# Squaring on ScalarE and adding a mask by matmul in a fused attention and mixture-of-experts kernel

## The chip, the cores and the metric

One Trainium2 chip, one core. The metric is the device time of one execution in microseconds; each figure for a kernel is the median of its runs.

## The reference

The function has three parts in a row, all in float32 at the interface.

1. Windowed attention over q, k, v of shape (4, 8, 576, 64): scores are q times k transposed over sqrt(64), a position sees itself and the 63 before it, everything else is masked; softmax, then times v. The result is laid out as 2304 tokens of 512 values.
2. A dense block: `h = x @ w_in` (512 to 2048), `g = max(h, 0)**2`, `x = g @ w_out` (2048 to 512). Its two weight matrices come as 64-bit floats.
3. A routed block of 8 experts: a token whose `x @ w_skip` is above 0 goes to the expert with the largest of `x @ w_gate`, and gets `x + p * (max(x @ w1[e], 0) @ w2[e])`, p being the softmax of the gate at that expert; other tokens pass through.

## The kernel before

**Tiles.** There are 18 tiles t of 128 tokens; two make a chunk c of 256 tokens (nine chunks). Attention works on tiles and on groups g of four heads (two groups for each tile, four for each chunk). The dense block works in units (c, j): `l1(c, j)` computes a 256-wide slice j of the hidden layer for the 256 tokens of chunk c, and `l2(c, j)` adds its contribution to the two output accumulators of the chunk. There are 8 slices, so 72 units. Float32 products are made of three matmuls of rounded parts, "hi times hi", "hi times lo", "lo times hi" (`mm3`, L424 to L426), so each activation and each weight is split into a high part (type float32r) and the remainder.

**One unit.** `l1` runs 24 matmuls into one of two PSUM banks named `h`. ScalarE (ACT) takes the relu into `r` (L437), which frees the bank. Then ACT squares r into the high part `gh` (L443), VectorE (DVE) squares r in place (L444) and subtracts gh to give the low part `gl` (L445). `l2` runs two units later (12 matmuls of 512 columns, `acc`).

**One attention group.** `at_qk` runs four score matmuls of 128 columns each (L245) into one bank: one of the two banks `h` (printed as `s`) for the chunks 0 and 1, one of the two banks `a` from chunk 2 on. DVE then adds the mask, scales by -1/8 and takes the running minimum in one operation for each of the four heads (L257); its output goes to SBUF (`e`) and its minimum to `nmx`. ACT takes four exponentials from there with `nmx` as bias (L263), DVE adds 1e-9, inverts and scales (L266 to L269). `at_tr` transposes (L277), ACT copies (L279), `at_pv` multiplies by v (L295) and splits the result into `xt` (L303, L304). The groups of chunks 0 and 1 are numbered 0 to 7 below.

**Conversion of the dense weights.** `conv_next` handles one of 32 half-blocks: ACT scales the high words (L202), GpSimd (POOL) clips (L203), DVE shifts and merges the bits in three operations (L205, L207, L209), ACT casts to the high part (L214), POOL subtracts to the low part (L215) and the next load is issued. The first ones run among the attention of chunks 0 and 1; the others run one behind each half unit, while the units of chunks 0 and 1 alternate, and the attention of chunk 2 runs in the last units of that stage. From unit 16 on (chunks 2 to 8) no conversion is left.

**Order.** Each engine has one queue and runs it in order. Outside two stretches written by hand (the last units, and the experts) a planner orders the instructions of each engine by costs that it estimates. Masks are made on POOL by `setup_masks`, `mask_of(t)` picks the two 128-wide pieces for a tile; ten warm-up matmuls (L563) run before the first scores. SP's queue issues the loads.

Of the kernel before, what the change touches and what calls it, by code (L numbers as in the profile page):

```python
# [10 lines left out]
BF16 = mybir.dt.bfloat16  # L11
I32 = mybir.dt.int32
U32 = mybir.dt.uint32
AF = mybir.ActivationFunctionType
ALU = mybir.AluOpType
AX = mybir.AxisListType
# [3 lines left out]
P = 128  # L20
# [4 lines left out]
CT = 2  # L25
# [11 lines left out]
QK_H = (0, 1)  # L37
WARM = 10
NST = 3
LOADN = 3  # L40
EWS = (3, 0, 0)
LATE = (0,)
# [12 lines left out]
HUGE = 3.0e38  # L55
# [6 lines left out]
def body(ctx, tc, qt_d, kt_d, vw_d, wi_d, wo_d, w9_d, w9r_d, w1_d, w2_d, out):  # L62
    nc = tc.nc
    pool = lambda name, bufs, **kw: ctx.enter_context(tc.tile_pool(name=name, bufs=bufs, **kw))

    def scoped(*specs):
        stack = ExitStack()
        return [stack.enter_context(tc.tile_pool(name=n, bufs=b, **kw)) for n, b, kw in specs], stack
# [13 lines left out]
    (kv,), kv_stack = scoped(("kv", 1, {}))  # L82
    (st, kv2), st_stack = scoped(("st", NST, {}), ("kv2", 1, {}))
    kvs = (kv, kv2)
# [10 lines left out]
    def sm():  # L95
        return sp.tile([P, 512], F32, tag="sm", name="sm")

    ident = const.tile([P, P], F32, name="ident")
    mask = const.tile([P, 4, P], F32, name="mask")
    tri = const.tile([P, P], BF16, name="tri")  # L100
    ones = const.tile([P, P], BF16, name="ones")
    w9 = const.tile([P, KD, 10], F32, name="w9")
# [7 lines left out]

    def setup_masks():
        make_identity(nc, ident)
        nc.gpsimd.memset(mask, 0.0)
        for h0 in (0, 64):
            m = mask[h0:h0 + 64]
            for i in (0, 1, 3):
                nc.gpsimd.affine_select(
                    out=m[:, i, :], in_=m[:, i, :], pattern=[[1, P]], compare_op=ALU.is_gt,
                    fill=-HUGE, base=0, channel_multiplier=-1)
            nc.gpsimd.affine_select(  # L120
                out=m[:, 2, :], in_=m[:, 2, :], pattern=[[1, P]], compare_op=ALU.is_ge,
                fill=-HUGE, base=-WIN, channel_multiplier=0)
            nc.gpsimd.affine_select(
                out=m, in_=m, pattern=[[0, 4], [-1, P]], compare_op=ALU.is_ge,
                fill=-HUGE, base=WIN, channel_multiplier=1)

    def setup_routing():
        nc.gpsimd.memset(ones, 1.0)
        nc.gpsimd.memset(tri, 1.0)
        nc.gpsimd.affine_select(  # L130
            out=tri, in_=tri, pattern=[[1, P]], compare_op=ALU.is_gt,
            fill=0.0, base=0, channel_multiplier=-1)
        nc.gpsimd.iota(io8i, pattern=[[1, NE]], base=0, channel_multiplier=0)
        nc.gpsimd.tensor_copy(out=io8, in_=io8i)
        nc.gpsimd.iota(route[:, :, 0], pattern=[[P, NT]], base=0, channel_multiplier=1)
        nc.gpsimd.memset(ohsum[:, 0, :], 0.0)
        fill = sm().bitcast(I32)
        nc.gpsimd.memset(fill, FAR)
        nc.scalar.dma_start(
            out=tab_v.rearrange("p r c -> p (r c)"), in_=fill[:, 0:2 * ROW])  # L140
        nc.scalar.dma_start(out=w9, in_=w9_d)
# [3 lines left out]
    def half_of(t):  # L145
        return t % 2 if t < 3 * CT else 0
# [15 lines left out]
    def load_next(t, load):  # L162
        n = t + 2 if t < 3 * CT - 1 else t + 1
        if t != 3 * CT - 1 and n < NT:
            load(n)
# [51 lines left out]

    e_t = {}

    def mask_of(t):  # L220
        off = 0
        for blk in range(2):
            if (2 * t + blk) % (S // WIN) == 0:
                off = 2 if blk == 0 else 1
        return mask[:, off:off + 2, :].rearrange("p a b -> p (a b)")

    p_t, pt_t, xt_t = {}, {}, {}

    def bank(role, t, g):
        c, i = divmod(t, CT)  # L230
        if role == "qk" and c in QK_H:
            return ps_h.tile([P, 512], F32, tag="h", name="s")
        if role == "pv" and c < 2:
            p_ = acc_pool.get(c, ps_acc)
            return p_.tile([P, DM], F32, tag=f"acc{g}", name="xp")
        return psa()

    def at_qk(t, g):
        s = bank("qk", t, g)
        qp, k_ = qpad[half_of(t)], kt_t[t]  # L240
        for pi in range(2):
            for blk in range(2):
                u = 2 * pi + blk
                pr = 2 * g + pi
                nc.tensor.matmul(  # L245
                    s[:, u * P:(u + 1) * P],
                    lhsT=qp[:, 2 * pr + blk].rearrange("p a b -> p (a b)"),
                    rhs=k_[:, pr, 64 * blk:64 * blk + P],
                    start=True, stop=True)
        if g == 1:  # L250
            load_next(t, load_qk)
        ef = sm()
        e = ef.rearrange("p (a b) -> p a b", a=4)
        nmx = small.tile([P, 4], F32, tag="nmx", name="nmx")
        mk = mask_of(t)
        for u in range(4):
            nc.vector.tensor_tensor_reduce(  # L257
                out=e[:, u, :], in0=s[:, u * P:(u + 1) * P],
                in1=mk[:, u % 2 * P:(u % 2 + 1) * P], scale=-1.0 / 8.0, scalar=HUGE,
                op0=ALU.add, op1=ALU.min, accum_out=nmx[:, u:u + 1])  # L260
        sums = small.tile([P, 4], F32, tag="sum", name="sum")
        for u in range(4):
            nc.scalar.activation(  # L263
                out=e[:, u, :], in_=e[:, u, :], func=AF.Exp, bias=nmx[:, u:u + 1],
                scale=-1.0, accum_out=sums[:, u:u + 1])
        nc.vector.tensor_scalar(  # L266
            out=sums, in0=sums, scalar1=1e-9, scalar2=None, op0=ALU.add)
        nc.vector.reciprocal(out=sums, in_=sums)
        nc.vector.tensor_tensor(  # L269
            out=e, in0=e, in1=sums.unsqueeze(2).to_broadcast([P, 4, P]), op=ALU.mult)  # L270
        p_t[t, g] = e
# [151 lines left out]
    def mm3(out_ap, ah, al, bh, bl, start, stop):  # L423
        nc.tensor.matmul(out_ap, lhsT=ah, rhs=bh, start=start, stop=False)  # L424
        nc.tensor.matmul(out_ap, lhsT=ah, rhs=bl, start=False, stop=False)  # L425
        nc.tensor.matmul(out_ap, lhsT=al, rhs=bh, start=False, stop=stop)  # L426

    def l1(c, j):
        hp = ps_h.tile([P, 2, CTOK], F32, tag="h", name="h")
        xt = xt_t[c]  # L430
        for f in range(2):
            for k in range(KD):
                o = (k % 2) * 256 + f * P
                mm3(hp[:, f, :], wi_t[j, k // 2][:, 0, o:o + P], wi_t[j, k // 2][:, 1, o:o + P],
                    xt[:, 0, k, :], xt[:, 1, k, :], k == 0, k == KD - 1)
        r = rp.tile([P, 512], F32, tag="r", name="r")
        nc.scalar.activation(  # L437
            out=r, in_=hp.rearrange("p a b -> p (a b)"), func=AF.Relu)
        gh = gp.tile([P, 2, CTOK], F32R, tag="gh", name="gh")
        gl = gp.tile([P, 2, CTOK], F32R, tag="gl", name="gl")  # L440
        ghf = gh.rearrange("p a b -> p (a b)")
        glf = gl.rearrange("p a b -> p (a b)")
        nc.scalar.activation(out=ghf, in_=r, func=AF.Square)  # L443
        nc.vector.tensor_tensor(out=r, in0=r, in1=r, op=ALU.mult)  # L444
        nc.vector.tensor_tensor(out=glf, in0=r, in1=ghf.bitcast(F32), op=ALU.subtract)  # L445
        g_t[c, j] = (gh, gl)

# [91 lines left out]
    for c in range(NCH - 1):  # L539
        base = last[c] + LAG  # L540
        for i in range(2):
            t = c * CT + i
# [9 lines left out]
    if True:  # L552
# [17 lines left out]
        for _ in range(LOOK - 2):  # L570
            conv_load()
        setup_masks()
        setup_routing()
        acc_pool[1] = ps_s
# [31 lines left out]
        for u in range(n_u):  # L606
            if u == first[2]:
# [5 lines left out]
                    out=w9b, in_=w9r_d.unsqueeze(0).to_broadcast([P, NE + 1, DM]))  # L613
# [32 lines left out]
        def gather(ti, gw, kind, i=0, rows=NTOK):  # L646
            xg = xg_t[kind][i % len(xg_t[kind])]
            ins = nc.gpsimd.indirect_dma_start(
                out=xg, out_offset=None, in_=x2_d[0:rows],
                in_offset=bass.IndirectOffsetOnAxis(ap=ti, axis=0),  # L650
                bounds_check=rows - 1, oob_is_err=False)
            return ti, gw, xg, ins
# [11 lines left out]
        early = gather(near[:, 0:1], None, 2, rows=(NT - CT) * P)[2]  # L664
# [40 lines left out]
        with tc.manual_schedule():  # L705
# [13 lines left out]
            for _ in range(EWS[1]):  # L719
# [25 lines left out]
                out=id0, in0=pick, scalar1=float(FAR), scalar2=nearf, op0=ALU.add, op1=ALU.min)  # L745
# [4 lines left out]
                out=cnt, in0=pc[:, 0:NE], scalar1=float(P - 1), scalar2=None, op0=ALU.add)  # L750
            nc.vector.tensor_scalar(
                out=cnt, in0=cnt, scalar1=7, scalar2=None, op0=ALU.logical_shift_right)
# [98 lines left out]
        def static(e, xt):  # L851
            def fill(i):
                n, m = FILLS[i]
                if i == LOADN and e + 1 < NE:
                    for x in range(e + (e > 0), e + 2):
# [73 lines left out]
```

## Time and profile before

| what | value |
|---|---|
| runs | 708.15, 708.60, 708.81 us, median 708.6 |
| span of the profiled execution, first to last instruction | 705.2 us |
| PE, matmul busy | 659.6 us (94%) |
| DVE busy | 486.3 us (69%) |
| ACT busy | 307.8 us (44%) |
| POOL busy | 160.0 us (23%) |

The profile shows one execution. For it the trace gives the span alone; the runs are 3.4 us longer at the median, for what lies before the first and after the last instruction. Busy times are sums over instructions; PE's are overlapped and modelled at their ends, so that a busy PE is not one at its peak. [...]

### The profile page before, as it was taken

The page shows a single profiled execution, that of the slowest core. Times are in us where ns is not written, and L with a number is a line of the kernel's source. Part 1 is how long each engine was busy: PE and PEld are TensorE (multiplying, and loading weights), DVE is VectorE, ACT ScalarE, POOL GpSimd, SP SyncE. Part 2 cuts the span into 40 slices and gives each one's busy share as a digit, 9 for nine tenths or more (in the row PEclk, how much of TensorE's full clock was granted, in tenths as well). Part 3 has the DMA queues.
Part 4 walks back from the last instruction along what each step waited for, and adds up shares of the span by engine and source line. Part 5 has one row for each costly group of instructions (what it writes and reads, how often), then busy time and mean ns, then how long its engine had stood idle before and what let it go on. Part 6 is the DMA issues. An engine that isn't in the chain of part 4 may idle for free. (4 is left out here: it accounts for less than half of the span.)

```text
span 705.2 us, 12314 instructions
## 1 busy us (share of the span) xinstructions
PE 659.6 (94%) x4461; PEld 571.9 (81%) x4461; DVE 486.3 (69%) x1354; ACT 307.8 (44%) x729; POOL 160.0 (23%) x181
## 2 busy tenths in 40 slices
PE   6699798899999999999999999999999898998786
PEld 4588687679998989989989989889988676776564
DVE  5989999967937836935945945954755363399871
ACT  4775535443434424334334334344442352476541
POOL 5556555510100000000000000030011432226420
PEclk9889999999999999999999999999999999999998
DMA  8964543344123123022122121116335644288820
GB/s 288 265 214 140 166 128 122 113 127 166 35 66 98 38 61 98 31 68 78 51 68 78 51 68 66 62 61 238 122 115 190 218 153 141 73 287 323 284 72 8
DMA packets 51076, 88.70 MB, mean 126 GB/s; under 512 B 24046, under 2 KB 24302, under 8 KB 50864
## 3 DMA queue, kind: packets, MB, share of 16 engines
q1 hardware_dynamic: 47584, 83.38, 35.6%
q0 software_dynamic: 2976, 3.95, 1.7%
q8 instruction: 46, 0.75, 0.4%
q10 hardware_dynamic: 432, 0.32, 0.1%
q14 instruction: 38, 0.31, 0.1%
HBM read 79.07 MB, written 12.49 MB: 130 GB/s over the span
## 5 line engine op out<-in xcount | busy, mean ns | idle before, releaser
L424 PE MATMUL h<-xt,wi 128*128 128x256 f32 x576 | 166.5, 290 | 5.1 <-ACT r L437 3.1
L426 PE MATMUL h<-xt,wi 128*128 128x256 f32 x576 | 165.1, 288 | 0.0
L425 PE MATMUL h<-xt,wi 128*128 128x256 f32 x576 | 164.4, 287 | 0.0
L424 PEld LDWEIGHTS h<-xt,wi 128*128 128x128 f32 x576 | 111.4, 193 | 9.5 <-ACT r L437 4.1
L424 PE MATMUL acc<-wo,gh 128*128 128x512 f32 x288 | 115.7, 406 | 2.5 <-ACT wo L214 2.5
L426 PE MATMUL acc<-wo,gl 128*128 128x512 f32 x288 | 112.7, 393 | 1.4 <-DVE gl L445 1.4
L425 PE MATMUL acc<-wo,gh 128*128 128x512 f32 x288 | 113.6, 394 | 0.0
L425 PEld LDWEIGHTS h<-xt,wi 128*128 128x128 f32 x576 | 111.5, 194 | 2.5
L426 PEld LDWEIGHTS h<-xt,wi 128*128 128x128 f32 x576 | 111.5, 194 | 0.4
L444 DVE TENSOR_TENSOR r<-r 128x512 f32<-128x512 f32 x72 | 53.5, 744 | 62.2 <-ACT gh L443 62.0
L437 ACT ACTIVATE r<-h 128x512 f32<-128x512 f32 x72 | 42.3, 593 | 115.6 <-PE h L426 113.3
L506 DVE TENSOR_TENSOR e<-r,e 128x1024 fp32r<-128x1024 f32 x58 | 73.3, 1283 | 28.0 <-ACT e L504 21.5
L416 POOL DMA_INDIRECT tab_d<-route,posi x18 | 19.5, 1086 | 314.7 <-DVE mx L356 182.5
L335 DVE CUSTOM_DVE_ANT_0 prod<-sm,w9b 128x512 f32<-128x512 f32 x108 | 74.1, 686 | 0.2
L504 ACT CAST e<-r 128x1024 fp32r<-128x1024 f32 x58 | 59.6, 1050 | 27.6 <-PE h L426 14.4
L263 ACT ACTIVATE sm<-sm,nmx 128x128 f32<-128x128 f32 x144 | 56.1, 392 | 26.6 <-DVE nmx L257 25.1
L426 PEld LDWEIGHTS acc<-wo,gl 128*128 128x128 f32 x288 | 54.1, 188 | 13.4 <-DVE gl L445 2.1
L424 PEld LDWEIGHTS acc<-wo,gh 128*128 128x128 f32 x288 | 54.0, 189 | 12.4 <-ACT wo L214 3.4
L774 PE MATMUL h<-e,xh 128*128 128x512 f32 x176 | 49.4, 410 | 13.0 <-issue 6.6
L425 PEld LDWEIGHTS acc<-wo,gh 128*128 128x128 f32 x288 | 54.4, 189 | 8.4
L445 DVE TENSOR_TENSOR gl<-r,gh 128x512 fp32r<-128x512 f32 x72 | 53.3, 741 | 1.9
L774 PEld LDWEIGHTS h<-e,xh 128*128 128x128 f32 x176 | 31.9, 191 | 23.3 <-issue 14.9
(158 smaller groups left out, 1065.0 us busy)
## 6 DMA issues: line engine op xcount, KB each, us to landing
r<-in_w_dram SPq DMA_DIRECT2D x64, 512.0 KB, 5.4
v<-in_vw_dram SPq DMA_DIRECT2D x18, 512.0 KB, 3.6
ri<-in_wi_dram SPq DMA_DIRECT2D x16, 512.0 KB, 4.0
ro<-in_wo_dram SPq DMA_DIRECT2D x16, 512.0 KB, 3.5
k<-in_kt_dram SPq DMA_DIRECT2D x18, 384.0 KB, 3.9
qpad<-in_qt_dram SPq DMA_DIRECT2D x36, 128.0 KB, 3.2
x_d<-sm SPq DMA_DIRECT2D x17, 256.0 KB, 2.6
out_dram<-sm SPq DMA_DIRECT2D x17, 256.0 KB, 3.0
```

Source lines behind the costliest of these rows:

```text
L263: nc.scalar.activation(out=e[:, u, :], in_=e[:, u, :], func=AF.Exp, bias=nmx[:, u:u + 1], scale=-1.0, accum_out=sums[:, u:u + 1])
L335: nc.vector.tensor_tensor_reduce(out=prod, in0=x2_t[t], in1=w9b_t[0][:, j, :], scale=1.0, scalar=0.0, op0=ALU.mult, op1=ALU.add, accum_out ...
L416: nc.gpsimd.indirect_dma_start(out=tab_d, out_offset=bass.IndirectOffsetOnAxis(ap=posi, axis=0), in_=route[:, t, :], in_offset=None, bound ...
L424: nc.tensor.matmul(out_ap, lhsT=ah, rhs=bh, start=start, stop=False)
L425: nc.tensor.matmul(out_ap, lhsT=ah, rhs=bl, start=False, stop=False)
L426: nc.tensor.matmul(out_ap, lhsT=al, rhs=bh, start=False, stop=stop)
L437: nc.scalar.activation(out=r, in_=hp.rearrange("p a b -> p (a b)"), func=AF.Relu)
L444: nc.vector.tensor_tensor(out=r, in0=r, in1=r, op=ALU.mult)
L445: nc.vector.tensor_tensor(out=glf, in0=r, in1=ghf.bitcast(F32), op=ALU.subtract)
L504: nc.scalar.copy(out=hi, in_=raw)
L506: eng.tensor_tensor(out=lo, in0=raw, in1=hi.bitcast(F32), op=ALU.subtract)
L774: nc.tensor.matmul(hp[f], lhsT=xt[a][:, k * P:(k + 1) * P], rhs=w1_t[e, k][b][:, f * 512:(f + 1) * 512], start=(i == 0), stop=(i == len(m1 ...
```

## The change

In `l1` the DVE multiply is removed; ACT squares r in place and then copies r into gh with rounding. For chunks 0 to 2 (`EARLY`) a bf16 matmul of the identity with a bf16 mask writes the mask into the score bank first, the four score matmuls add to it, one DVE maximum reads the bank, ACT scales it by 1/8, and the exponentials read the bank. From chunk 3 on attention stays as it was, with a float32 mask now copied from the bf16 one.

```diff
+EARLY = (0, 1, 2)
...
+    identb = kv2.tile([P, P], BF16, name="identb")
     mask = const.tile([P, 4, P], F32, name="mask")
+    maskb = kv2.tile([P, 4, P], BF16, name="maskb")
...
         make_identity(nc, ident)
-        nc.gpsimd.memset(mask, 0.0)
+        nc.gpsimd.tensor_copy(out=identb, in_=ident)
+        nc.gpsimd.memset(maskb, 0.0)
         for h0 in (0, 64):
-            m = mask[h0:h0 + 64]
+            m = maskb[h0:h0 + 64]
...
+        nc.gpsimd.tensor_copy(
+            out=mask.rearrange("p a b -> p (a b)"), in_=maskb.rearrange("p a b -> p (a b)"))
...
-    def mask_of(t):
+    def mask_of(t, m):
...
-        return mask[:, off:off + 2, :].rearrange("p a b -> p (a b)")
+        return m[:, off:off + 2, :].rearrange("p a b -> p (a b)")
...
         qp, k_ = qpad[half_of(t)], kt_t[t]
+        early = t // CT in EARLY
+        if early:
+            nc.tensor.matmul(
+                s.rearrange("p (a b) -> p a b", a=2), lhsT=identb,
+                rhs=mask_of(t, maskb).unsqueeze(1).to_broadcast([P, 2, 2 * P]),
+                start=True, stop=False, skip_group_check=True)
...
-                    start=True, stop=True)
+                    start=not early, stop=True, skip_group_check=early)
...
-        mk = mask_of(t)
-        for u in range(4):
-            nc.vector.tensor_tensor_reduce(
-                out=e[:, u, :], in0=s[:, u * P:(u + 1) * P],
-                in1=mk[:, u % 2 * P:(u % 2 + 1) * P], scale=-1.0 / 8.0, scalar=HUGE,
-                op0=ALU.add, op1=ALU.min, accum_out=nmx[:, u:u + 1])
+        if early:
+            nc.vector.tensor_reduce(
+                out=nmx, in_=s.rearrange("p (a b) -> p a b", a=4), axis=AX.X, op=ALU.max,
+                negate=True)
+            nc.scalar.mul(nmx, nmx, 1.0 / 8.0)
+        else:
+            mk = mask_of(t, mask)
+            for u in range(4):
+                nc.vector.tensor_tensor_reduce(
+                    out=e[:, u, :], in0=s[:, u * P:(u + 1) * P],
+                    in1=mk[:, u % 2 * P:(u % 2 + 1) * P], scale=-1.0 / 8.0, scalar=HUGE,
+                    op0=ALU.add, op1=ALU.min, accum_out=nmx[:, u:u + 1])
...
             nc.scalar.activation(
-                out=e[:, u, :], in_=e[:, u, :], func=AF.Exp, bias=nmx[:, u:u + 1],
-                scale=-1.0, accum_out=sums[:, u:u + 1])
+                out=e[:, u, :], in_=s[:, u * P:(u + 1) * P] if early else e[:, u, :],
+                func=AF.Exp, bias=nmx[:, u:u + 1],
+                scale=1.0 / 8.0 if early else -1.0, accum_out=sums[:, u:u + 1])
...
-        nc.scalar.activation(out=ghf, in_=r, func=AF.Square)
-        nc.vector.tensor_tensor(out=r, in0=r, in1=r, op=ALU.mult)
+        nc.scalar.activation(out=r, in_=r, func=AF.Square)
+        nc.scalar.copy(out=ghf, in_=r)
         nc.vector.tensor_tensor(out=glf, in0=r, in1=ghf.bitcast(F32), op=ALU.subtract)
```

## Rows read from the trace of the kernel before

**Rows 1.** The page, busy time, share of the span and instructions of each engine.
```profile
PE 659.6 (94%) x4461; PEld 571.9 (81%) x4461; DVE 486.3 (69%) x1354; ACT 307.8 (44%) x729; POOL 160.0 (23%) x181
```
**Rows 2.** Windows: length; busy PE, PEld, DVE, ACT, POOL; PEclk; DMA share; GB/s.
```profile
20.00:43.60 23.60, 18.34 (x139) 16.14 (x140) 21.82 (x68) 16.22 (x55) 12.81 (x15) 0.71 0.82 250
43.60:94.30 50.70, 46.63 (x326) 42.05 (x326) 49.12 (x77) 28.21 (x63) 29.78 (x39) 0.97 0.49 160
94.30:142.70 48.40, 42.97 (x283) 36.03 (x281) 47.72 (x72) 24.05 (x55) 27.87 (x32) 1.00 0.35 119
...
150.00:545.00 395.00, 394.87 (x2942) 356.81 (x2941) 253.83 (x985) 151.99 (x415) 26.25 (x31) 1.00 0.27 89
```
**Rows 3.** Waits of PE, DVE, ACT, 20 to 150 us: total, times, longest.
```profile
PE a L277 <- DVE sum L266: 4.2, 2, 2.2
PE h L424 <- ACT r L437: 3.1, 2, 1.7
PE acc L424 <- ACT wo L214: 2.5, 3, 1.9
PE a L277 <- DVE sm L269: 2.5, 2, 1.6
...
PE h L424 <- DVE nmx L257: 0.5, 1, 0.5
...
DVE xt L304 <- ACT xt L303: 2.8, 4, 1.3
...
ACT wo L214 <- DVE f L209: 25.9, 13, 4.3
ACT wi L214 <- DVE f L209: 15.5, 9, 3.4
```
**Rows 4.** DVE by line, 20 to 145 us: count, busy, mean ns, idle before.
```profile
L444 DVE TENSOR_TENSOR r<-r 128x512 f32<-128x512 f32 x13 | 12.9, 995 | 0.9 <-ACT gh L443 0.9
L445 DVE TENSOR_TENSOR gl<-r,gh 128x512 fp32r<-128x512 f32 x13 | 11.7, 898 | 0.2
```
**Rows 5.** DVE by line, 150 to 530 us.
```profile
L444 DVE TENSOR_TENSOR r<-r 128x512 f32<-128x512 f32 x57 | 39.3, 689 | 61.2 <-ACT gh L443 61.0
...
L312 DVE COPY sm<-acc 128x512 f32<-128x512 f32 x9 | 6.2, 687 | 1.9 <-PE acc L426 1.9
```
**Rows 6.** ACT by line, 20 to 145 us; the last row 150 to 530 us.
```profile
L443 ACT ACTIVATE gh<-r 128x512 fp32r<-128x512 f32 x15 | 9.3, 634 | 0.0
...
L376 ACT ACTIVATE sh<-sh 128x8 f32<-128x8 f32 x16 | 3.3, 208 | 2.2 <-DVE sh L373 2.2
```
**Rows 7.** Windows of line L257 alone: DVE's busy time.
```profile
20.00:43.60 23.60, 3.67 (x32) 0.71 0.82 250
43.60:142.70 99.10, 3.83 (x32) 0.98 0.42 140
```
**Rows 8.** Timeline around the first layer-1 matmul: start, duration, instruction.
```profile
37.27 0.58 PE L424 MATMUL h<-xt,wi 128*128 128x256 f32 x1 [0.51 <-DVE nmx L257]
...
38.33 0.39 ACT L263 ACTIVATE sm<-sm,nmx 128x128 f32<-128x128 f32 x1
```
**Rows 9.** Timeline: warm-up matmuls, and two layer-2 matmuls at full clock.
```profile
1.30 4.11 PE L563 MATMUL a<-sm 128*128 128x512 bf16 x10 [1.30 <-DVE sm L555]
...
77.95 0.39 PE L424 MATMUL acc<-wo,gh 128*128 128x512 f32 x1
78.18 0.39 PE L425 MATMUL acc<-wo,gh 128*128 128x512 f32 x1
```
**Rows 10.** Timeline of the start.
```profile
5.04 1.33 POOL L123 TENSOR_SCALAR_AFFINE_SELECT mask<-mask 64x512 f32<-64x512 f32 x2
...
5.99 2.02 PE L245 MATMUL s<-k,qpad 128*128 128x128 f32 x16 [0.58 <-DMA k<-in_kt_dram]
...
9.39 0.66 ACT L202 ACTIVATE ri<-ri 128x512 f32<-128x512 f32 x1 [6.66 <-DMA ri<-in_wi_dram]
```
**Rows 11.** Windows, 80 to 90 us, columns as in rows 2.
```profile
80.00:90.00 10.00, 6.55 (x38) 5.91 (x37) 9.79 (x12) 3.48 (x7) 5.75 (x8) 0.84 0.37 122
```

## The prediction

> **What bounds the kernel now.** I read the page's first two parts, then busy time by stage, then the waits of each engine inside the stage that looked odd. Over the whole span TensorE (PE) is busy 94% and VectorE (DVE) 69% [rows 1], which taken alone says that relieving DVE is worth nothing. The stages say otherwise [rows 2]. From 150 to 545 us PE is busy 394.87 of 395 us: there the matmuls are the bound. In 20 to 43.6, 43.6 to 94.3 and 94.3 to 142.7 us DVE is busy 21.82 of 23.60, 49.12 of 50.70 and 47.72 of 48.40 us, while PE leaves 5.26, 4.07 and 5.43 us empty. This is the stage in which the 32 half-blocks of first- and second-layer weights are converted from 64-bit floats, three DVE operations each.
>
> The waits of 20 to 150 us confirm it [rows 3, 4]. DVE waited 2.8 us for ScalarE's (ACT's) copy of xt and 0.9 us for gh, and for nothing else; ACT waited 25.9 and 15.5 us for DVE's converted words (L209) before its casts; PE's waits are for DVE directly, or for ACT operations that queue behind those casts (relu L437, cast L214). An in-order DVE queue that is always busy sets the pace here. What is taken off it shortens the stage, until PE has no empty time left. The end of the chain of waits, in the expert stage after 545 us, isn't touched by the edits.
>
> **The squares.** Each of the 72 units (one 256-wide slice of the hidden layer for 256 tokens) loses the DVE multiply L444. Before, ACT squared r into gh, and DVE squared r again in place; now ACT squares in place and copies to gh, so ACT gains one 512-wide operation per unit and DVE loses one. In 20 to 145 us 13 multiplies took 12.9 us, mean 995 ns [rows 4]; in 150 to 530 us, with GpSimd (POOL) almost idle, 57 took 39.3 us, mean 689 ns [rows 5]. POOL was busy 29.78 and 27.87 us in the two later conversion windows [rows 2], so some 0.3 us of each 995 ns is time in which the multiply was slowed beside POOL. Does that part go too? If it goes, the gain on DVE is 12.9 us. If the slowing passes to the next operation in the queue, it is 13 x 0.689 = 9.0 us. Instructions also overlap by about 0.09 us (start to start some 0.60), which makes 13 x 0.60 = 7.8 us the low end. I take 9.0: POOL's work does not shrink, and L445, also of two inputs, was slowed beside it as well (mean 898 ns [rows 4]).
>
> [...]
>
> After 150 us the other 57 multiplies save nothing: DVE sat idle 61.0 us in front of them [rows 5] and PE has no gap. The ACT operation put in costs about 0.60 us (a square of this size took 634 ns [rows 6], and they overlap a little). ACT is busy 28.21 of 50.7 and 24.05 of 48.4 us in the conversion windows [rows 2]; 13 more make about 8 us over the two, some 61% busy. It stays hidden, but gh is ready some 0.6 us later, while gl, which waited for square, multiply and subtract, comes out about even (0.60 for 0.69). The second layer uses both two units (some 12 us) later. After 150 us ACT rises from 152 to about 187 of 395 us, behind PE's full queue.
>
> **The mask, DVE side.** In chunks 0 to 2, 12 groups of scores lose four 128-wide add-and-minimum operations each (L257, with an accumulator read behind each) and get one 512-wide maximum from PSUM. The eight groups inside 20 to 142.7 us cost 3.67 + 3.83 = 7.5 us of DVE [rows 7]. The maximum isn't in the trace; the nearest row is a 512-wide DVE copy from PSUM, 687 ns [rows 5], so 8 x 0.687 = 5.5 us and 2.0 us saved. Bounds: no gain (four times the 0.28 us of one 128-wide operation, without their overlap, is 1.1 us, more than the 0.94 of a group now), and 3.5 us if one takes 0.5 us. Half of the 2.0 falls before 43.6 us, half after.
>
> **The mask, ACT and PSUM side.** Each early group adds one 128x4 scale on ACT (0.2 us; a 128x8 activation takes 208 ns [rows 6]), and its four exponentials now read the scores in PSUM. So a score bank comes free after the last exponential, not after the last DVE operation. The place where this shows is the first layer-1 matmul: it started at 37.27 us, just after the DVE had finished with the bank of group 6, and waited 0.5 us for that [rows 3, 8]. The last exponential of that group starts at 38.33 us and takes 0.39 [rows 8]. With the scale, PE's first unit would start up to 1.9 us later; what is late next is relu and DVE's first subtraction at some 45 us. DVE has other work in its queue meanwhile, and also gets 1.0 us back before that point: I take +1.0 us for the wait (0 to 1.9) against the -1.0 of DVE.
>
> **The mask, PE side.** 12 matmuls of 512 bf16 columns are added. The trace has this shape in the warm-up: 10 in 4.1 us, 0.41 us each; a 512-wide layer-2 matmul starts 0.23 us after the one before it at full clock [rows 9]. Eight fall before 43.6 us, where PE has gaps; four, of chunk 2, between 95 and 143 us, at 0.23 to 0.41 us: 0.9 to 1.6, and I take 0.9.
>
> **The masks at the start.** POOL now writes a bf16 mask, a bf16 identity and a float copy, and the first score matmul needs the first two. Before, the mask's last select started at 5.04 us and ran 1.33, the first score matmul started at 5.99, waiting for the DMA of k, and the first exponential came behind an ACT conversion at 9.39 that waited for its DMA [rows 10]. Half a microsecond on POOL is covered by these 2 to 3 us: nothing, at worst 1 us. The DMAs on SP's queue keep their number.
>
> **The sum.** Between 43.6 and 142.7 us DVE loses 9.0 + 1.0 = 10.0 us, and PE has 4.07 + 5.43 = 9.5 us empty. So PE caps the gain, and it can't get all: in the first window 3.45 of its 4.07 us lie in 80 to 90 us [rows 11], where it ran out of converted weights; I count 3.5 there, and 4.5 of the 5.43 in the second, 8.0 in all. Before 43.6 us -1.0 and +1.0 cancel; +0.9 for the matmuls. That is -7.1 us: a span of 698.1 after 705.2. The trace gives no other time of its execution; the median of the runs is 708.6, 3.4 us over the span, which I take as unchanged: **701.5 us**. Its own range is 697.5 to 705: 7.8 instead of 9.0 on DVE, no gain from the maximum and +1.9 for the bank make it some 3.5 worse; the end at 697.5 is that of PE's gaps used up, below.
>
> **The rivals.** *More than that:* DVE gets the slowed part back too (12.9 + 1.0), and PE uses up its 9.5 us. [...] -11.1 + 0.9 gives 698.4, with a cheap maximum up to 2 less: 696 to 698.5. For it speaks that DVE is full to 97%; against it that PE would then have to run the stage without one gap, fed by two queues that wait for one another.
>
> *No change:* the gain is given back. PE is in the window 43.6 to 94.3 already 92% busy; if its gaps are the start-up of each weight block (DMA, ACT, POOL, DVE, ACT, POOL in a row) and not DVE's load, DVE gets idle time instead of a shorter stage. Against it: DVE waits only 3.7 us in 130 [rows 3, 4], so it is hardly ever short of input. 707.2 to 710.
>
> *Slower, ACT's queue becomes the bound:* relu frees one of two layer-1 banks, and it sits in ACT's in-order queue behind casts that wait for DVE (41.4 us in all). The copy put into that queue pushes each following relu back by 0.6 us; PE already waited 3.1 us for relu [rows 3]. It decides if the relu is late in more units than DVE's relief makes early: with 13 late by 0.6 us, 7.8 us, and of DVE's gain only about half of PE's direct waits for DVE (7.2 us [rows 3]) left, some 4, the time is 708.6 + 7.8 - 4 + 0.9 = 713; a mix ends at 710 to 713. Against it: ACT would be only 61% busy, and its waits shrink as DVE gets ahead. The order of the queues is the planner's and can change with the new costs, which is why I don't put this lower. [...]
>
> **Chances.** Forecast 0.62, more 0.14, no change 0.11, slower 0.13. Beyond 0.2% (1.4 us, about what a measurement of this kernel tells from no change): faster 0.76, same 0.11, slower 0.13. The range for 8 in 10, 695.5 to 708.5, leaves out the slower case and a little at the lower end.
>
> **What would show it.** Right: the stage before the first routing work (the window that ended at 142.7 us) ends some 7 us earlier; PE's empty time in it falls from 9.5 to below 3 us; PE stays full up to some 538 us; the operation of L444 is gone from DVE, with ACT's waits for L209 well under 41 us; the maximum takes near 0.69 us. The bank term is right if the first layer-1 matmul waits for an exponential. Wrong: DVE idle in the conversion stage while PE still waits; long waits of PE for relu; a PE that is not full after 150 us; or a changed expert stage, which I take as 160 us long either way.

## The result, and the profile after

The changed kernel takes 712.98 us (median of 4 runs, 711.34 to 714.64) against 708.38 for the kernel before in the same session: a ratio of 1.0063, 95% interval 1.0040 to 1.0086. It is slower by 4.6 us, where 7 us less was forecast. The span of its profiled execution is 709.6 us; that execution took 711.34, so 1.7 us lie outside the span (the 3.4 between the span before and its median hold a difference between executions as well). First the page, busy time of each engine, and the granted clock of PE (PEclk, the share of full speed that it was granted; here in tenths, in 40 slices of 17.7 us):

```profile
PE 661.8 (93%) x4473; PEld 573.8 (81%) x4473; DVE 442.6 (62%) x1198; ACT 350.4 (49%) x813; POOL 157.9 (22%) x183
...
PEclk9899999999999999999999999999999999989998
```

DVE lost 43.7 us of work and ACT gained 42.6 [rows 1], as the edit says. To see where the time went, I compare marks that exist in both executions: the first matmul of layer-1 unit 16 (the end of the conversion stage), and the first and the last matmul of the experts. They are read from the timeline by counting matmuls of a line (24 in a unit).

| mark, us from the start | before | after | difference |
|---|---|---|---|
| first layer-1 matmul | 37.27 | 36.98 | -0.3 |
| unit 16 starts | 151.97 | 145.10 | -6.9 |
| last layer-2 matmul starts | 532.97 | 525.92 | -7.05 |
| first expert matmul | 540.71 | 533.64 | -7.1 |
| 6th expert block starts | 609.77 | 604.35 | -5.4 |
| 7th expert block starts | 622.63 | 622.15 | -0.5 |
| last expert matmul starts | 697.88 | 702.33 | +4.45 |

So the forecast gain of 7.1 us is there, complete, at the first expert matmul, and 5.4 us of it still at the sixth expert block. Then it is lost: the experts, whose code the edit doesn't touch, take 168.69 us where they took 157.17. Windows from the first to the last expert matmul, before and then after (length; busy PE, PEld, DVE, ACT, POOL; PEclk; DMA share; GB/s):

```profile
540.71:697.88 157.17, 141.82 (x659) 110.22 (x657) 96.08 (x97) 73.15 (x99) 52.48 (x35) 0.99 0.52 180
```
```profile
533.64:702.33 168.69, 146.35 (x660) 114.32 (x657) 95.38 (x97) 73.26 (x99) 51.24 (x35) 0.95 0.50 168
```

The work is the same. PE's empty time is 22.3 us where it was 15.4, and its busy time is 4.5 us longer at a mean granted clock of 0.95 for 0.99. That is the 11.5 us: 7.0 empty, 4.5 of slower matmuls at the lower clock. (The matmuls of L793 that read xh, which come first behind a jump, took 444 ns in the mean where they had taken 410; those that write y took 396 in both.) PE's weight loads behind the sixth and the seventh executed expert block show the empty time (timeline of PEld, after):

```profile
615.79 0.87 PEld L818 LDWEIGHTS y<-e,hl 128*128 128x128 f32 x4
622.15 3.06 PEld L793 LDWEIGHTS h<-e,xh 128*128 128x128 f32 x8 [5.50 <-issue]
...
635.79 0.87 PEld L818 LDWEIGHTS y<-e,hl 128*128 128x128 f32 x4
640.18 1.87 PEld L793 LDWEIGHTS h<-e,xh 128*128 128x128 f32 x6 [3.53 <-issue]
```

and in the kernel before, behind the seventh block:

```profile
635.01 0.87 PEld L799 LDWEIGHTS y<-e,hl 128*128 128x128 f32 x4
636.42 1.45 PEld L774 LDWEIGHTS h<-e,xh 128*128 128x128 f32 x7 [0.54 <-issue]
639.58 0.19 PEld L774 LDWEIGHTS h<-e,xh 128*128 128x128 f32 x1 [1.72 <-issue]
```

Between the first line and the next of each pair lies a jump: a branch on the number of tokens (L839 before, L858 after) skips the code of further blocks that this expert doesn't need. After it the changed kernel's PE does nothing for 5.5 and 3.5 us; the kernel before runs on after 0.5 us and stops for 1.7 us seven weight loads later. It stops in this way behind its sixth, eighth and ninth block too, after ten, four and one weight loads (the first of these stops is 1.2 us long), and behind the tenth at the jump itself:

```profile
650.82 0.76 PEld L774 LDWEIGHTS h<-e,xh 128*128 128x128 f32 x4 [0.54 <-issue]
654.44 0.76 PEld L774 LDWEIGHTS h<-e,xh 128*128 128x128 f32 x4 [2.87 <-issue]
...
666.37 0.19 PEld L774 LDWEIGHTS h<-e,xh 128*128 128x128 f32 x1 [0.54 <-issue]
669.70 1.94 PEld L774 LDWEIGHTS h<-e,xh 128*128 128x128 f32 x7 [3.14 <-issue]
...
686.02 1.68 PEld L774 LDWEIGHTS h<-e,xh 128*128 128x128 f32 x8 [2.69 <-issue]
```

"issue" means that PE waited for nothing which the profile shows: no semaphore, no data. What the DMA view shows in the first gap of the changed kernel, beside the experts' weights (q1), is a transfer of instructions (617 to 622.2 us: packets, MB, share):

```profile
q1 hardware_dynamic: 564, 1.09, 57.0%
q8 instruction: 1, 0.02, 1.2%
q14 instruction: 2, 0.02, 0.7%
```

Over the kernel q8 moved 46 packets with 0.75 MB, 16 KB each, and in either kernel one of them runs in, or reaches into, the gap behind each of the last five jumps; only the one of the kernel before at 623.63 us ends 0.1 us ahead of its gap. In the waits of PE from 545 us on, the changed kernel has 17.9 us of "issue" and of PE's own sequencer (PEq) at that branch (first two rows), the kernel before 10.6 (last two rows):

```profile
PE h L793 <- PEq L858: 11.7, 5, 3.1
PE h L793 <- issue: 6.2, 2, 5.1
```
```profile
PE h L774 <- issue: 7.3, 4, 2.8
PE h L774 <- PEq L839: 3.3, 2, 2.3
```

### The profile page after: what moved, and what is told of

Same layout as the page of the kernel before. It is cut to its first block, busy times and chain, and to the rows that moved or that the text cites. A ratio compares the mean times of both kernels' runs of the same rounds, so it can differ in the third digit from the quotient of the medians.

```text
span 709.6 us, 12278 instructions
## 1 busy us (share of the span) xinstructions
PE 661.8 (93%) x4473; PEld 573.8 (81%) x4473; DVE 442.6 (62%) x1198; ACT 350.4 (49%) x813; POOL 157.9 (22%) x183
## 5 line engine op out<-in xcount | busy, mean ns | idle before, releaser
L445 PE MATMUL h<-xt,wi 128*128 128x256 f32 x576 | 164.0, 285 | 0.0
L445 PE MATMUL acc<-wo,gl 128*128 128x512 f32 x288 | 112.5, 392 | 0.0
L445 PEld LDWEIGHTS h<-xt,wi 128*128 128x128 f32 x576 | 110.7, 192 | 0.5 <-POOL wi L221 0.2
L464 DVE TENSOR_TENSOR gl<-r,gh 128x512 fp32r<-128x512 f32 x72 | 54.2, 752 | 85.7 <-ACT gh L463 85.5
L525 DVE TENSOR_TENSOR e<-r,e 128x1024 fp32r<-128x1024 f32 x58 | 69.8, 1222 | 41.1 <-ACT e L523 38.9
L456 ACT ACTIVATE r<-h 128x512 f32<-128x512 f32 x72 | 42.5, 594 | 80.7 <-PE h L445 78.3
L793 PE MATMUL h<-e,xh 128*128 128x512 f32 x176 | 54.0, 444 | 20.5 <-PEq L858 11.7
L445 PEld LDWEIGHTS acc<-wo,gl 128*128 128x128 f32 x288 | 54.1, 188 | 11.7
L793 PEld LDWEIGHTS h<-e,xh 128*128 128x128 f32 x176 | 34.9, 209 | 31.2 <-issue 21.6
L281 ACT ACTIVATE sm<-sm,nmx 128x128 f32<-128x128 f32 x96 | 37.5, 392 | 20.7 <-DVE nmx L275 20.3
L798 ACT ACTIVATE r<-h 128x512 f32<-128x512 f32 x22 | 13.2, 600 | 68.3 <-PE h L793 68.3
```

Source lines behind the costliest of these rows:

```text
L281: nc.scalar.activation(out=e[:, u, :], in_=s[:, u * P:(u + 1) * P] if early else e[:, u, :], func=AF.Exp, bias=nmx[:, u:u + 1], scale=1.0 ...
L456: nc.scalar.activation(out=r, in_=hp.rearrange("p a b -> p (a b)"), func=AF.Relu)
L525: eng.tensor_tensor(out=lo, in0=raw, in1=hi.bitcast(F32), op=ALU.subtract)
L793: nc.tensor.matmul(hp[f], lhsT=xt[a][:, k * P:(k + 1) * P], rhs=w1_t[e, k][b][:, f * 512:(f + 1) * 512], start=(i == 0), stop=(i == len(m1 ...
L798: nc.scalar.activation(out=rs[f], in_=hp[f], func=AF.Relu)
```

## The experiments

**Theory A.** The change puts 12 matmuls, 24 instructions with their weight loads, into TensorE's program ahead of the experts, and drops a few waits: the expert code starts 20 instructions later (the traces record 85 semaphore instructions of TensorE ahead of the first branch before, 81 after: 24 less 4). Code is loaded in pieces, by this theory the 16 KB packets of q8, and where a jump's target lies within its piece decides whether PE waits at the jump, a little later, or not at all. **Theory B.** The experts' weights arrive otherwise, or ScalarE's added work or the mask part itself is to blame.

The tiny keep-warm matmuls (`keep_warm`, 128 columns, 219 ns each, 58 in all at 535 to 541 us) make a test possible: they stand ahead of the experts, fill waits, and nothing reads them. Adding or dropping one moves TensorE's expert code by 2 instructions.

**1. The kernel before with only its code shifted.**
```diff
-KEEP = (14, 20, 12, 12)
+KEEP = (16, 24, 14, 14)
```


> The kernel before with ten more of the tiny keep-warm matmuls (58 become 68) ahead of the experts, and nothing else: it moves TensorE's expert code 20 instructions further, as far as the change moves it, and adds about 0.6 us of filler where TensorE waits anyway. Theory A (the changed kernel lost its gain because TensorE's code for the experts starts 20 instructions later, so that the loading of code falls on the jumps): the expert stage, from the first expert matmul to the last, grows from 157 to some 168 us, the time is 716 to 721 us, and the half-clock stretches of 620 to 680 us show here too. Theory B (the weights' transfers and the other engines' changed work cause it): the stage stays at 157 us and the time at 708 to 709.5.

720.2 us, ratio 1.0165 (1.0130 to 1.0200). The expert stage takes 171.49 us, with the waits of the changed kernel at the jumps:

```profile
PE h L774 <- PEq L839: 12.0, 5, 3.1
PE h L774 <- issue: 4.9, 2, 3.4
```

Neither edit of the change is in this kernel. Theory B falls for the bulk of the loss.

**2. The changed kernel with its code put back.**
```diff
-KEEP = (14, 20, 12, 12)
+KEEP = (12, 16, 10, 10)
```


> The changed kernel with ten keep-warm matmuls fewer (48), which puts TensorE's expert code back to the position that it has in the kernel before. Theory A: the conversion stage keeps its gain of 7 us and the expert stage goes back to about 157 us: 700 to 703 us. Theory B: nothing moves, 712 to 714 us.

702.83 us, ratio 0.9933 (0.9907 to 0.9959); expert stage 159.58 us. The time is within 1.4 us of the forecast one. Against the kernel before of the same session it is 4.7 us less, not 7.1: unit 16 starts 6.3 us earlier, and the first five expert blocks take 71.6 us where they took 69.1. The last six take 88.0 us, as before (88.1).

**3. The square alone.** The diff of `l1`, on the kernel before.

> The kernel before with the square on ScalarE alone; the mask stays with VectorE. TensorE's expert code lies 6 instructions earlier than before. By my sum the squares are 9 of the 11 us taken off VectorE: layer 1 of unit 16 starts 5 to 7 us before 151.97. Theory A: the expert stage is not longer than 157 to 159 us, so 701 to 704 us. Theory B, with ScalarE's added work as the cause in the experts: the stage is near 168 us and the time 711 to 715.

701.87 us, ratio 0.9902 (0.9866 to 0.9937). Unit 16 starts at 144.87 us, 7.1 before 151.97: the whole gain of the conversion stage. The expert stage takes 161.08 us, some 2 more than expected.

**4. The mask alone.** All of the change but the lines in `l1`.

> The changed kernel with the square undone (VectorE multiplies again), so the mask part alone. TensorE's expert code lies 22 instructions later than before, 2 later than in the changed kernel. By my sum the conversion stage gains 0 to 2 us. Theory A: the expert stage is as long as in the changed kernel, near 168 us, and the time is 716 to 721 us. Theory B with ScalarE's square as the cause: 706 to 709 us.

721.18 us, ratio 1.0171 (1.0133 to 1.0210). Unit 16 starts at 152.06, so the mask part gains nothing there, and the expert stage takes 175.08 us, 7 longer than expected: its last six blocks take 98.7 us, as in the changed kernel (98.0), its first five 76.3 (70.7 there).

**5. The mask alone, with its code put back** (`KEEP` 47 in all).

> The mask part alone, with 11 keep-warm matmuls fewer, so that the expert code lies exactly where it lies before. Theory A: what is left is what the mask part does by itself in the conversion stage, which ended at 152.06 us against 151.97: 707 to 710 us. Rival, the mask part costs time by itself in the experts: 716 us or more.

706.08 us, ratio 0.9971 (0.9941 to 1.0001), below the range that I gave, and not to be told from no change. So what the mask part alone cost in experiment 4, some 14 us, went with the place of the code.

**6. The kernel before with its code 40 instructions earlier.**
```diff
-KEEP = (14, 20, 12, 12)
+KEEP = (9, 14, 8, 7)
```


> The kernel before with 20 keep-warm matmuls fewer (38 instead of 58): TensorE's expert code starts 40 instructions earlier. Theory A, refined: behind each jump over skipped code TensorE runs as far as the code that is already loaded reaches, then waits for the next 16 KB. Before, that reach was 11, 8, 5, 2 and 0 weight loads in the last five jumps; 40 instructions earlier it is about 20 more each, some 4 us of work, more than the 3.3 us that a wait at the jump itself took. So the waits of 1.2 to 3.1 us behind the last five jumps go, and the stage falls from 157 to 146 to 150 us: 698 to 702 us in all. Rival: a shift only moves the waits about, or fewer keep-warm matmuls cost a half-clock stretch at 535 us: 706 to 711 us.

698.17 us, ratio 0.9840 (0.9808 to 0.9872): some 11 us for taking out 20 matmuls that nothing reads. The expert stage takes 149.04 us, and the stop behind the jump has gone (PEld, the same place):

```profile
636.00 0.89 PEld L799 LDWEIGHTS y<-e,hl 128*128 128x128 f32 x4
637.43 1.67 PEld L774 LDWEIGHTS h<-e,xh 128*128 128x128 f32 x8 [0.55 <-issue]
639.14 0.87 PEld L774 LDWEIGHTS h<-e,xl 128*128 128x128 f32 x4
640.05 0.87 PEld L774 LDWEIGHTS h<-e,xh 128*128 128x128 f32 x4
```

In the window of its experts PE is empty for 7.5 us (149.04 less 141.57), half of before:

```profile
540.30:689.34 149.04, 141.57 (x655) 110.19 (x656) 95.20 (x97) 73.73 (x99) 51.23 (x35) 0.99 0.54 190
```

**7 and 8. The square with its code 41 and 81 instructions earlier** (`KEEP` 38 and 18 in all).

> The square on ScalarE alone, with 20 keep-warm matmuls fewer: expert code 46 instructions earlier than before. Theory A: the 7 us of the conversion stage and the 8 to 11 us of the jumps add up: 691 to 696 us. Rival: no better than the square alone, 700 to 703 us.

> The square on ScalarE alone, with 40 keep-warm matmuls fewer (18 left): expert code 86 instructions earlier than before. Theory A: the waits behind the jumps are gone already at 46, so 690 to 696 us again, unless the missing filler lowers TensorE's clock around 535 us (then 2 to 3 us more). Rival: each place has its own waits, anything from 692 to 705 us.

695.02 us (0.9783, 0.9743 to 0.9823) and 695.62 us (0.9799, 0.9758 to 0.9841), expert stages 152.39 and 153.32 us. There is a broad good place, not a single lucky one.

**9. One block of code more.**
```diff
         for _ in range(WARM):
             nc.tensor.matmul(warm, lhsT=dummy[:, 0:P], rhs=dummy[:, 0:512], start=True, stop=True)
+        for _ in range(108):
+            nc.tensor.matmul(
+                warm[:, 0:1], lhsT=dummy[:, 0:P], rhs=dummy[:, 0:1], start=True, stop=True)
```


> The kernel before with 108 one-column matmuls behind the warm-up: 216 instructions more, 2 of them covered by waits that the build drops, so the expert code lies 214 later, that is 42 earlier than before but one block of 16 KB (256 instructions) on. The extra matmuls delay the first scores by some 5 to 10 us, so only the expert stage counts here. Theory A, it is the place within the 16 KB block that matters: from the first expert matmul to the last 147 to 151 us, as with 40 instructions fewer. Rival, more code ahead always costs: 165 us or more.

The expert stage takes 148.60 us, as with 40 instructions fewer (149.04), though there are 216 more: 256 less 40, the same place in the next piece. The number of keep-warm matmuls is unchanged here, so it is not their number that shortened the stage in experiment 6. The one run took 698.74 us, since the conversion stage, bound by DVE, swallowed the late start (unit 0 at 41.67, unit 16 at 152.43 us). So it is the place within a piece of 256 instructions that counts. The traces have the same number: from 144.43 to 517.34 us of the kernel before, where PE is never empty, q8 moved 22 packets of 16 KB while TensorE started 5626 recorded instructions (2787 matmuls, as many weight loads, and semaphore instructions), 256 to a packet; in the changed kernel it was 5619 in 22, from 154.85 to 529.83 us.

**10. The code 60 instructions later** (`KEEP` 88 in all).

> The kernel before with 30 keep-warm matmuls more: expert code 60 instructions later than before, 40 later than in the first shifted kernel. Theory A: the jumps land in a block that is not yet loaded, as at 20, and wait about 3.3 us each, no more: expert stage 166 to 175 us, 715 to 723 us in all. Rival, the cost grows with the shift: above 725 us.

719.55 us in one run, expert stage 168.93 us: no worse than at 20. By theory A the jumps of both places land in a piece that is not loaded; they cost the same, 3.3 to 3.8 us at the first four of the last five jumps, and 2.3 and 2.4 at the last one (PEld):

```profile
646.89 3.06 PEld L774 LDWEIGHTS h<-e,xh 128*128 128x128 f32 x8 [3.42 <-issue]
```

**11. The whole change with its code 40 instructions earlier** (`KEEP` 28 in all).

> The changed kernel, square and mask, with 30 keep-warm matmuls fewer (28 left), so that the expert code starts 40 instructions earlier than before, as in the run of the kernel before with early code. Theory A: 7 us from the conversion stage and about 10 from the experts: 691 to 696 us, level with the square alone at early code (the mask part adds nothing). Rival, the mask part is worth its 2 us once the code lies well: 689 to 692.5 us.

692.79 us, ratio 0.9796 (0.9747 to 0.9845), the fastest by its median and 20 us below the change as it was made. It can't be told from the square alone at early code (0.9783).

All runs, by where TensorE's expert code lies:

| kernel | code, instructions against before | unit 16 starts | expert stage | its last six blocks | median us |
|---|---|---|---|---|---|
| square | -81 | 145.95 | 153.32 | 77.9 | 695.62 |
| square | -41 | 146.30 | 152.39 | 78.7 | 695.02 |
| square and mask | -40 | 145.20 | 152.08 | 79.1 | 692.79 |
| before | -40 | 151.56 | 149.04 | 77.7 | 698.17 |
| square | -1 | 144.87 | 161.08 | 89.6 | 701.87 |
| mask | -1 | 150.87 | 158.84 | 87.9 | 706.08 |
| before | 0 | 151.97 | 157.17 | 88.1 | 708.38 |
| square and mask | 0 | 145.70 | 159.58 | 88.0 | 702.83 |
| square and mask (the change) | +20 | 145.10 | 168.69 | 98.0 | 712.98 |
| before | +20 | 151.35 | 171.49 | 97.0 | 720.20 |
| mask | +21 | 152.06 | 175.08 | 98.7 | 721.18 |
| before | +60 | 151.75 | 168.93 | 96.7 | 719.55 |
| before | +216 | 152.43 | 148.60 | 79.0 | 698.74 |

The place is counted in the traces: 2 instructions for each matmul ahead of the first branch, and TensorE's semaphore instructions there (85 before, 84 with the square alone, 82 with the mask alone, 81 with both). The expectations of experiments 3, 4, 5, 7, 8 and 9 state other places (6 earlier, 22 later, exactly as before, 46 and 86 earlier, 214 later); by the traces they are those of the table. The stage times are those of the one profiled execution of each kernel.

The third column depends on the square: 145 to 146 us with it, 151 to 152 without. The last six blocks depend on the place of the code: 78 to 79 us from -81 to -40 and at +216, 88 to 90 at -1 and 0, 97 to 99 from +20 to +60, with either edit or none. The first five blocks, 69 to 76 us, don't follow it.

## Why the prediction was wrong

**What bounds the stage: right. The sum for it: right in part by luck.** DVE was the bound from 20 to 143 us. Forecast -8.0 us in that stage and -7.1 in all up to the experts; measured -6.9 at unit 16 with both parts, -7.1 with the square alone. The windows of the changed kernel, against [rows 2]:

```profile
20.00:43.60 23.60, 17.98 (x170) 15.62 (x167) 22.64 (x41) 17.32 (x64) 12.38 (x17) 0.87 0.88 271
43.60:94.30 50.70, 47.92 (x329) 43.00 (x329) 47.83 (x58) 33.82 (x75) 30.97 (x40) 0.97 0.51 164
94.30:135.80 41.50, 38.04 (x253) 33.16 (x252) 39.94 (x50) 26.41 (x62) 24.42 (x29) 1.00 0.33 108
...
150.00:538.00 388.00, 387.88 (x2900) 350.55 (x2900) 217.67 (x915) 183.73 (x461) 27.16 (x31) 1.00 0.27 86
```

DVE is still full (47.83 of 50.70, 39.94 of 41.50), ACT's waits for L209 (now L215) fell from 41.4 to 25.2 us, and PE stays full after 150 us with ACT at 184 us, as forecast. One sign failed, and a step of the sum with it. The sum took the gain out of PE's empty time, 8.0 of 9.5 us; in the two later windows that fell to 6.2 us only, not below 3. From the first layer-1 matmul to unit 16, in the kernel before, the changed one, and the changed one with its code put back:

```profile
37.27:151.97 114.70, 104.58 (x720) 91.05 (x721) 109.18 (x178) 62.40 (x145) 62.95 (x74) 0.96 0.39 131
36.98:145.10 108.12, 101.17 (x729) 89.35 (x725) 99.86 (x126) 69.46 (x160) 61.52 (x74) 0.98 0.43 140
37.44:145.70 108.26, 99.91 (x728) 87.99 (x724) 100.04 (x126) 69.44 (x160) 60.72 (x74) 1.00 0.44 141
```

PE's empty time fell by 3.2 us, and its busy time by 3.4, at a granted clock of 0.98 for 0.96: a term that the sum doesn't have (a rival had it). The third row has the full clock, less busy time and more empty time, and the same length. So PE's empty time was what DVE's pace left over, and no cap on the gain. The rival's 11.1 us, which the range's end of 697.5 also takes in, are the 9.5 of empty time and an estimate of 1.6 for the granted clock of 0.84 in 80 to 90 us (0.50 from 87 to 90 us). No run shows those 1.6 us as time gained: the second and the third row differ by 1.3 us of busy time, at 0.98 and 1.00, and are equally long. DVE's own account is this: its busy time fell by 9.3 us, where 10.0 were counted, and its idle time grew by 2.7, because it now waits for gh, behind square and copy on ACT; the prediction had counted that as about even (waits of 20 to 155 us after, of 20 to 150 before):

```profile
DVE gl L464 <- ACT gh L463: 5.3, 8, 1.3
```
```profile
DVE r L444 <- ACT gh L443: 0.9, 2, 0.5
```

9.3 less 2.7 is the 6.6 us by which this stretch is shorter. That the cap of 8.0, less 0.9 for the matmuls, came to nearly the same is luck.

**The mask: right in sum, not in its terms.** The maximum took 0.68 us for 0.687 (DVE lines, 20 to 145 us):

```profile
L288 DVE TENSOR_TENSOR sm<-sm,sum 128x512 f32<-128x512 f32 x10 | 10.6, 1062 | 0.1
L285 DVE TENSOR_SCALAR sum<-sum 128x4 f32<-128x4 f32 x9 | 4.3, 477 | 0.8 <-ACT sm L281 0.8
L268 DVE TENSOR_REDUCE nmx<-a 128x4 f32<-128x512 f32 x4 | 2.7, 680 | 0.0
L268 DVE TENSOR_REDUCE nmx<-s 128x4 f32<-128x512 f32 x4 | 2.7, 678 | 0.0
```

That is 5.4 us for the 7.5 of the operations removed. But the scaling of the exponentials (L288, before L269) took a mean of 1062 ns where it had taken 717, and the small sum (L285, before L266) 477 where it had taken 158. Those two grew by 3.4 and 2.9 us, more than the 2.1 saved. They grew with the mask alone too (1086 and 398 ns), so the square isn't needed for it. That they now fall beside POOL's conversions is my reading of it; no run isolates it. It fits the choice made for the squares, that slowed time passes to the next operation, which was an estimate; the subtraction (L464, before L445) took a mean of 972 ns in this window, where it had taken 898. The waiting for a bank, +1.0 in the sum, did not occur where I put it: the first layer-1 matmul started at 36.98 us with no wait before it. PE waited for the exponentials at mask matmuls instead (0 to 70 us):

```profile
PE s L249 <- ACT sm L281: 3.9, 3, 2.1
```

Two of these three waits lie before 20 us, and unit 0 started no later for them. At unit 16 the mask part is worth +0.1 and -1.1 us in its two runs.

**The step that failed** is the last clause: "a changed expert stage, which I take as 160 us long either way", with the remark that the edits don't touch that stage. It took 168.69 us after 157.17, and 171.49 with nothing but the shift. I priced the 12 added matmuls by the time they run (0.9 us) and not by the 24 instructions they add ahead of the branches. Moved by 20 instructions, the targets of the last jumps lay, by theory A, outside the piece of code that was already loaded, and PE's weight loads stood at each of these jumps, for 2.1 to 5.5 us. Before, PE had still run 10, 7, 4, 1 and 0 weight loads behind the last five jumps, ever fewer, before it stopped (the expectation of experiment 6 counts one too many in the first four). In both kernels at -1 it ran 11, 8, 5, 2 and 0: one instruction moved the wait by one load. The kernel before stood at the edge, and its trace showed this, in waits called "issue" behind L839, which I passed over as they named no engine. None of my rivals had this mechanism. The one that ended on the right side, ACT's queue as the bound, was wrong: PE waited 2.4 us for relu in the conversion stage, where it had waited 3.1.

**The clock.** The granted clock of PE in the changed kernel is 0.66 in the window from 620 to 630 us: it fell in the 5 us without a matmul, from 1.00 (619 to 620 us) to 0.50 (621 to 622), and was still at 0.50 when the matmuls began again (622 to 626). It is lower again behind the next three gaps (0.83 from 640 to 650 us, 0.88 from 650 to 660, 0.83 from 670 to 680), but not behind the last (1.00 from 690 to 700):

```profile
620.00:630.00 10.00, 7.85 (x26) 6.18 (x27) 3.58 (x4) 2.52 (x4) 2.62 (x2) 0.66 0.69 242
```

These stretches are where I put the 4.5 us of longer busy time. In the kernel before it fell once in the experts (0.83 in the window from 670 to 680 us).

**What stays open.** The first five expert blocks differ by 5.6 us between two kernels whose code lies one instruction apart (the change, 70.7, and the mask alone, 76.3). Of these, 4.2 us are busy time of PE, at a granted clock of 0.93 where the change had 1.00; the rest is empty time. The kernel before and the change kept the full clock there (1.00 from 540.71 to 609.77 and from 533.64 to 604.35 us), and the kernel at +216 had 1.00 over its whole expert stage; over theirs the two kernels at -40 had 0.99, the change with its code put back 0.98, and the kernel before at +20 0.93. What makes the clock fall in one and not in the other, and how much of it changes from one execution to the next, I haven't settled. The square alone is 2.4 us longer than the kernel before in the first five blocks and 1.5 in the last six.

## What to carry to other kernels

A change ahead of branches is also a change of where the code behind them lies; before judging it, compare the stages that it doesn't touch, and if one of them moved, shift the code alone (a few instructions that nothing reads) and time that. Gaps of an engine with no releaser, just behind a jump and with a transfer of instructions in them, are time to be had by moving the code: here some 11 us of 708, more than the 7 that the edit itself was worth. A price by stage came out within a microsecond here, in part by luck, and still gave the wrong sign for the whole.

## What the runs showed of the hardware

Behind the first four of the last five jumps TensorE's weight loads were idle for 3.2 to 3.9 us in the four kernels at +20, +21 and +60 (5.5 once); in these gaps of the changed kernel q8 started a 16 KB packet of instructions, and the weights' queue took 57 to 71% of the DMA engines. At the last jump, where in the changed kernel no weights were moving any more, it was 2.1 to 2.4 us; whether the one comes from the other wasn't tested. Where weight loads ran on behind the jump, the pause at it was 0.54 us in the kernel before, and 0.55 in the one at -40. TensorE went through 256 recorded instructions for each 16 KB packet of q8 (5626 in 22), and 216 instructions more and 40 fewer, which are 256 apart, gave the same stage, 148.6 and 149.0 us. In the changed kernel the granted clock of PE was 0.50 from 621 to 626, 641 to 644, 658 to 661 and 675 to 678 us, at the end of or behind the gaps of 3.2 to 5.5 us, and 1.00 behind the last one, of 2.1 us. On DVE a 512-wide maximum from PSUM took 680 ns, as a copy of that size does (687).
